# The last batch's output product by seven block products instead of eight, in an attention and gated projection kernel

## The chip, the cores and the metric

The kernel runs on one core of one Trainium2 chip. The metric is the time on the device in microseconds. The engines are PE (TensorE: matrix products), DVE (VectorE), ACT (ScalarE), POOL (GpSimd) and SP (SyncE, which issues most DMAs). "PEld" is PE's load of weights, which runs beside its products.

## The reference

```python
# q, k, v: (8 batches, 12 heads, 448 tokens, 64); x: (8, 448, 768)
scores = scale * q @ k.T - log(S)
attn = sigmoid(scores) @ v             # its heads side by side are x
gate = sigmoid(causal convolution of x over the tokens, 5 taps, each channel by itself)
val = x @ w_val                        # 768 x 768
out = (gate * val) @ w_out             # 768 x 768
```

All is float32.

## The kernel before

Everything is kept transposed: a row of 128 partitions holds 128 channels, and the columns are tokens. The 768 channels are six blocks, c for the summed side and m for the side that comes out. The tokens of batch 0 are spread over batches 1 to 7, so those have T = 448 + 64 = 512 columns each and batch 0 needs no products of its own.

The 48 pairs of heads are worked on in 24 steps j of two pairs each: scores on PE, a sigmoid on ACT (L552), scaling to float16 parts on ACT (`a`, L367) and DVE (L563), the product with v on PE (L602, L610). Three steps make a batch. The convolution (`tap`, `gate`) runs on ACT and DVE, with sums made by DMAs that POOL issues (L683).

A projection to near float32 accuracy is made of float16 numbers: each operand is a high part and a low part, and each 128 x 128 block takes three matmuls, hi by hi, hi by lo and lo by hi (L753). So a product for one m is 6 x 3 = 18 matmuls of 512 columns, summed in one of two PSUM banks (`ps_m`). For `val`, DVE multiplies the result with the gate (`y`, L777), a cast gives its high part and a difference its low part (`g`); for `out`, ACT or DVE scales the result (`y`) and two DMAs write it (L785 and L786). The last `out` product of the last batch is made in two halves of 256 columns (L759 to L769), so that the first half is written earlier. Weights come as 64-bit words, are made float32 in a buffer of the `words` ring (three buffers), get a power of two as scale from their largest value (`weight_sum`, a matmul with one column, L421; `exponent`), and are split (`weight_split`).

The order of the instructions isn't the order of the code. Each piece of work is an `op` with the engines that can do it, a cost on each, the buffers that it reads and writes, and a due time; the table AT holds the numbers that due times are made of. `Plan.issue` (L179) goes through a modelled time and gives each engine that comes free the ready op with the earliest due time. What comes out is one fixed list for each engine, and on the chip an engine executes its list in order. Buffers come from rings: an op that takes a buffer waits for the last reader of its former content.

After the last attention step PE has only products to do: `out` of batch 6, `val` of batch 7, `out` of batch 7, six column blocks each.

Of the kernel before, what the change touches and what calls it, by code (L numbers as in the profile page):

```python
# [58 lines left out]
VAL_SCALE = 2.0**-17  # L59
# [11 lines left out]
BY_GPSIMD = ()  # L71


# [5 lines left out]
    first=6.63, step=13.72, val=-77.5, val_step=60.94, out=57.5, out_step=597.15, w_max=-57.5,  # L79
    w_split=-155, load_qk_first=-152, load_qk=69.5, load_v=-40.5, split_hi=-2, split_lo=30,  # L80
    rest_first=95.5, rest=251, a_first=-174.5, a=-7, attend=-47.5, v_max=76.5, v_exp=14.5,
    v_split=-159.5, x=-174.5, x_max=-98, x_scale=-307, x_hi=52.5, x_lo=-185.5, x_step=2940.66, tap=51,
    scores=68.5, a_rest=85, a_rest_first=-72.5, tap_first=22, tap_pair=68.5, tap_step=56.18, gate=-110,
    product=63.5, y=-61.5, g_hi=186.5, g_lo=6, o=-97, share=0.3, w_load=-117,
# [172 lines left out]
def attention_then_gate(  # L257
# [101 lines left out]
    def copy(eng, to, x):  # L359
        if eng == "A":  # L360
            nc.scalar.copy(to, x)  # L361
        else:
            nc.vector.tensor_copy(to, x)
# [30 lines left out]
    def exponent(e, read, cols, prio, po=None):  # L394
# [24 lines left out]
    def weight_sum(n, m):  # L419
        b = w_max[n][m]  # L420
        return [b, ones], lambda to: mm(to[:, m : m + 1], ones(), b()[:, m : m + 1], start=True, stop=True)  # L421
# [313 lines left out]

    gv = {}

    def product(n, b, m):
        t = tau((b + 1) * NP) + AT["product"] + (m + NC * (n == "out")) * STEP / 2
# [19 lines left out]
        if (n, b, m) == ("out", B - 1, NC - 1):  # L759

            y = y_ring.new()
            for k, (low, cs) in enumerate(((y, slice(0, T // 2)), (y.part(), slice(T // 2, T)))):
# [4 lines left out]
                op({"S": 0.45}, t + k, lambda e, cs=cs: nc.sync.dma_start(out[b, m, :, cs], y()[:, cs]), [low], [], P * 1000)
            op({"S": 0.45}, t + 2, lambda e: nc.sync.dma_start(out[0, m, :, S - SL :], y()[:, S:]), [low], [], P * 1000)
# [70 lines left out]
    for j in range(TWOS):  # L839
        for i in (2 * j, 2 * j + 1):  # L840
            if i < len(columns):
                weight(*columns[i])
# [15 lines left out]
        if j + 1 < TWOS:  # L858
# [89 lines left out]
```

## Time and profile before

| | us |
|---|---|
| median of 3 runs | 579.45 |
| lowest and highest | 578.76, 580.03 |
| span of the profiled execution | 578.0 |
| PE busy | 571.4 |
| DVE busy | 428.4 |
| ACT busy | 435.4 |
| POOL busy | 138.2 |

The span is that of one profiled execution, from its first to its last instruction. A row of the timeline has start and duration in us, engine, line of the kernel, operation, output and inputs, shapes, and a count when neighbours are drawn together; in brackets stands the idle time before it and what ended that. In a group of instructions the first number behind the bar is their busy time in us, the second the mean of one in ns, the third the idle time before them. Matmuls are pipelined, so that their durations overlap: the pitch from start to start says what one costs.

### The profile page before, as it was taken

What the parts mean: (1) busy time and instruction counts of PE and PEld (TensorE: products, weight loads), DVE (VectorE), ACT (ScalarE), POOL (GpSimd) and SP (SyncE); (2) the same over time, 40 slices, a digit from 0 to 9 for tenths busy, and PEclk for the clock granted to TensorE, in tenths of its full rate; (3) what the DMA queues carried; (4) which work ended last, traced back from release to release, by engine and by line L of the source; (5) the groups of instructions that cost most, each with busy time, mean ns of one, the idle gap of its engine ahead of it and who ended that gap; (6) DMA issues with size and microseconds to landing.
All of it is one profiled execution on the core that took longest, in us unless ns stands there. A gap on an engine that the chain in (4) does not pass through costs nothing.

```text
span 578.0 us, 9459 instructions
## 1 busy us (share of the span) xinstructions
PE 571.4 (99%) x3592; PEld 280.2 (48%) x3592; DVE 428.4 (74%) x693; ACT 435.4 (75%) x579; POOL 138.2 (24%) x162
## 2 busy tenths in 40 slices
PE   9999999999999999999999999999999999999997
PEld 5343334455555555545555454554545555544444
DVE  1867999899977959888598886889777886760310
ACT  5677988879888869778697878788788897862112
POOL 0000203332424222243322333223322322110000
PEclk9999999999999999999999999999999999999999
DMA  8988677757484564825657364565635663355012
GB/s 327 355 279 267 174 210 188 203 120 184 124 215 83 146 157 141 207 58 155 136 158 176 102 169 96 166 156 155 169 74 168 155 133 74 72 128 129 2 37 74
DMA packets 39310, 88.44 MB, mean 153 GB/s; under 512 B 14944, under 2 KB 20448, under 8 KB 39264
## 3 DMA queue, kind: packets, MB, share of 16 engines
q0 software_dynamic: 8640, 31.46, 29.4%
q1 hardware_dynamic: 30624, 56.37, 28.9%
q8 instruction: 28, 0.46, 0.3%
q14 instruction: 18, 0.15, 0.1%
HBM read 43.96 MB, written 12.40 MB: 98 GB/s over the span
## 4 chain that ended last, share of the span: by engine, by line
PE 90%; DVE 5%; ACT 3%; DMA 1%; issue 1%; ACTq 0%; DVEq 0%
PE ps_m L753 54%; PE ps_a L516 15%; PE ps_a L610 14%; PE ps_a L539 3%; PE ps_a L602 2%; DMA gate<-tap 1%; ACT a_single L552 1%; DVE x_max L658 1%; DVE gate L679 1%; PE ps_m L800 1%; DVE a L563 1%; DVE w_words L389 1%; DVE out_max L415 0%; ACT tap L367 0%; ACT a L367 0%
## 5 line engine op out<-in xcount | busy, mean ns | idle before, releaser
L753 PE MATMUL ps_m<-g,w_out_hi 128*128 128x512 f16 (+1 forms) x516 | 150.5, 374 | 0.0
L753 PE MATMUL ps_m<-xs,w_val_hi 128*128 128x512 f16 x504 | 150.1, 379 | 0.0
L552 ACT ACTIVATE ps_a<-ps_a 128x896 f32<-128x896 f32 x112 | 99.3, 909 | 14.2 <-DVE v_exp L544 6.5
L563 DVE SCALAR_TENSOR_TENSOR a<-ps_a,a 128x896 f16<-128x896 f32 x96 | 100.8, 1082 | 7.0 <-ACT a L367 6.7
L372 POOL TENSOR_TENSOR qk_lo<-qk_src,qk_hi 128x448 fp32r<-128x448 f32 x66 | 75.2, 1151 | 119.8 <-ACT qk_hi L361 36.7
L753 PE MATMUL ps_m<-g,w_out_lo 128*128 128x512 f16 (+1 forms) x258 | 96.5, 374 | 0.0
L683 POOL DMA_DIRECT2D gate<-tap x60 | 53.5, 892 | 178.6 <-ACT tap L367 70.2
L753 PE MATMUL ps_m<-xs,w_val_lo 128*128 128x512 f16 x252 | 95.5, 379 | 0.0
L367 ACT ACTIVATE a<-ps_a 128x896 f16<-128x896 f32 x96 | 85.0, 927 | 0.2
L367 ACT ACTIVATE tap<-x,cw 128x512 f32<-128x512 f32 x120 | 82.2, 739 | 1.5 <-DMA gate<-tap 1.5
L753 PEld LDWEIGHTS <-w_out_hi 128*128 128x128 f16 x516 | 49.0, 98 | 59.6 <-issue 5.3
L753 PEld LDWEIGHTS <-w_val_hi 128*128 128x128 f16 x504 | 47.8, 98 | 61.1 <-issue 5.9
L777 DVE SCALAR_TENSOR_TENSOR y<-ps_m,y_scale,gate 128x512 f32<-128x512 f32 x42 | 29.9, 745 | 34.3 <-PE ps_m L753 34.3
L610 PE MATMUL ps_a<-a,v_hi 128*64 128x448 f16 x384 | 52.7, 354 | 0.0
L367 ACT ACTIVATE y<-ps_m,o_scale 128x512 f32<-128x512 f32 (+1 forms) x35 | 23.1, 678 | 38.0 <-PE ps_m L753 25.4
L552 ACT ACTIVATE a_single<-ps_a 128x896 f32<-128x896 f32 x56 | 48.0, 927 | 4.5 <-PE ps_a L516 4.1
L361 ACT CAST g<-y 128x512 f16<-128x512 f32 x28 | 17.2, 618 | 33.7 <-DVE y L777 32.9
L516 PE MATMUL ps_a<-qk_hi 64*128 64x448 f32 x198 | 39.8, 398 | 0.1
L753 PEld LDWEIGHTS <-w_out_lo 128*128 128x128 f16 x258 | 25.2, 98 | 29.2
L753 PEld LDWEIGHTS <-w_val_lo 128*128 128x128 f16 x252 | 24.7, 98 | 29.7
L516 PE MATMUL ps_a<-qk_single 64*128 64x448 f32 x180 | 39.0, 566 | 0.0
L610 PE MATMUL ps_a<-a_single,v_src 128*64 128x448 f32 x192 | 37.8, 543 | 0.0
(108 smaller groups left out, 752.9 us busy)
## 6 DMA issues: line engine op xcount, KB each, us to landing
gate<-tap POOLq DMA_DIRECT2D x60, 512.0 KB, 4.9
qk_src<-qk SPq DMA_DIRECT2D x33, 448.0 KB, 5.4
v_src<-vs SPq DMA_DIRECT2D x24, 448.0 KB, 4.3
out_t<-y SPq DMA_DIRECT2D x41, 224.0 KB, 3.1
qk_single<-qk SPq DMA_DIRECT2D x15, 448.0 KB, 5.9
w_words<-w_val SPq DMA_DIRECT2D x6, 768.0 KB, 8.1
w_words<-w_out SPq DMA_DIRECT2D x6, 768.0 KB, 5.4
x<-first_x SPq DMA_DIRECT2D x21, 68.0 KB, 4.2
```

The source lines that it names most:

```text
L361: nc.scalar.copy(to, x)
L367: nc.scalar.activation(to, x, AF.Copy, scale=by)
L372: engines[eng].tensor_tensor(to, x, y, op=ALU.subtract)
L516: mm(b()[:, h, :S], k()[rows, at : at + P], q()[rows, :S], start=(n == 0), stop=(n == len(terms(i)) - 1))
L539: mm(b()[to, h, :S], x[n]()[rows, CW:], x[n]()[rows, :S], start=True, stop=True)
L552: nc.scalar.activation(to, b()[:, :, :S], AF.Sigmoid, bias=-math.log(S), scale=1.0 / math.sqrt(D))
L563: op({"V": 1.0}, t + 0.5, lambda e: nc.vector.scalar_tensor_tensor(part(1), p(), A_SCALE, part(0), op0=ALU.mult, op1=ALU.subtract), [b], [ ...
L602: mm(px()[to, p, :S], v()[rows, h * D : (h + 1) * D], x(s["a"])[rows, h, at : at + S], start=(j > 0 and n == 0), stop=(j == 0 and n == len ...
L610: mm(px()[to, p, :S], v()[:, o : o + D], x(st[2 * j + p]["a", c])[:, h, at : at + S], start=(j == 0 and c == 0 and n == 0), stop=(j > 0 an ...
L683: op({"G": 1.1}, at + AT["tap_step"] * k, lambda e, tap=tap: nc.gpsimd.dma_start(g(), tap(), accum_op=ALU.add), [tap], [g], 4 * P * T * 4, "")
L753: mm(po()[:, cs], w()[:, c, :], x(k)[:, cs], start=(c == 0 and j == 0), stop=(c == NC - 1 and j == 2))
L777: op({"V": 0.66}, t + AT["y"], lambda e: nc.vector.scalar_tensor_tensor(y(), po(), y_scale()[:, m : m + 1], gate()[:, m % 2, :], op0=ALU.m ...
```

## The change

The tokens of the last batch are two halves of 256 columns, and the channels of the summed side (c even, c odd) and of the side that comes out (m even, m odd) are two blocks each. `out` of the last batch is then a 2 by 2 product of blocks, eight block products. The change makes it of seven (Strassen's algorithm):

- `mix(q)`, for each of the three pairs of column blocks of `w_out`: four sums and differences of blocks of weights, each 128 x 384, made from the high and low parts and split again. It takes a buffer of the `words` ring and two of the ring of `tap`. Its ops are due in mid-run (called at batch 4), on DVE, POOL and ACT. For this the two blocks of a pair share one scale (`weight_sum`: four matmuls of one column for a pair, instead of two).
- The last batch's `val` result is multiplied with the gate in place (L912). `form(b, q)` splits three blocks, adds blocks in place (four adds of 128x256, L813), and splits the four blocks that come out.
- `product_mixed(b)`: seven steps of three q of three c of three matmuls of 256 columns (L852), into both halves of a bank of `ps_a`, with an evacuation of 256 columns after each step of each q that scales and adds or subtracts (L871, L369), and DMAs to the output.
- Two `out` products of batch 6 (HELD_BACK = 2, m = 4 and 5) are due after `val` of batch 7.
- The table of due times is new throughout, due times are rounded to five digits, BY_GPSIMD (empty) is gone.

The core of the diff:

```diff
-VAL_SCALE = 2.0**-17
+VAL_SCALE = 2.0**-19
+OUT_TOP = 13
+HELD_BACK = 2
 AT = dict(
-    first=6.63, step=13.72, val=-77.5, val_step=60.94, out=57.5, out_step=597.15, w_max=-57.5,
+    first=-11.29, step=17.95, val=156.55, val_step=-46.86, out=18.08, out_step=-29.96, w_max=90.21,
...
+    w_load=192.46, mix=196.26, mix_step=-137.47, form=63.29, mixed=64.39, held=-170.35,
 )
...
     def weight_sum(n, m):
-        b = w_max[n][m]
-        return [b, ones], lambda to: mm(to[:, m : m + 1], ones(), b()[:, m : m + 1], start=True, stop=True)
+        b = w_max[n][m : m + (1 if n == "val" else 2)]
+
+        def emit(to):
+            for at in range(m, m + len(b)):
+                for k, x in enumerate(b):
+                    mm(to[:, at : at + 1], ones(), x()[:, m + k : m + k + 1], start=(k == 0), stop=(k == len(b) - 1))
...
+    def mix(q):
+        prio = AT["mix"] + AT["mix_step"] * q
+        f = mixed[q] = words.new(lambda: sb.tile([P, 8, NQ * P], F16, name="mixed", tag="w_words", bufs=WORDS))
+        t, u = tap_ring.new(), tap_ring.new()
...
+        def two_sub(to, k, a, b, at):
+            op({"G": 1.05, "V": 0.45}, prio + at, lambda e: sub(e, slot(to, k), block(0, *a), block(0, *b)), reads, [to])
+            op({"G": 1.05, "V": 0.45}, prio + at, lambda e: sub(e, slot(u, 1), block(1, *a), block(1, *b)), reads, [u])
+            op({"G": 1.05, "V": 0.45}, prio + at, lambda e: engines[e].tensor_tensor(
+                flat(to, k), flat(to, k), flat(u, 1), op=ALU.add), [u], [to])
...
+        def split(n, src, k, sign, at):
+            op({"A": 0.5, "V": 0.32}, prio + at, lambda e: scaled(e, hi(), flat(src, k), sign), [src], [part[n]])
...
+    def form(b, q):
+        g, t = st[b * NP + 2 * q]["g"], tau((b + 1) * NP) + AT["form"] + 2 * q
...
+            op({"A": 0.2 + 0.21 * n, "V": 0.1 + 0.16 * n}, t, lambda e, at=at, n=n, to=to: copy(
+                e, h()[:, to : to + n, :], blocks()[:, at:, :]), [g], [hb])
+            op({"V": 0.1 + 0.3 * n, "G": 0.2 + 0.62 * n}, t + 0.1, lambda e, at=at, n=n, to=to: sub(
+                e, l()[:, to : to + n, :], blocks()[:, at:, :], h()[:, to : to + n, :]), [g, hb], [lb])
+            if at:
+                def add(e):
+                    x = blocks()
+                    for a, by in ((2, 0), (0, 1), (1, 2), (3, 1)):
+                        engines[e].tensor_tensor(x[:, a, :], x[:, a, :], x[:, by, :], op=ALU.add)
+                op({"V": 1.5}, t + 0.2, add, [], [g])
...
+    def product_mixed(b):
+        steps = (
+            (0, 0, "B11", True), (1, 5, 0, True), (0, 4, 1, False), (1, 6, "B22", False), (0, 3, 2, False),
+            (1, 2, "B21", True), (0, 1, 3, False),
+        )
...
+                        for j, (a, src) in enumerate(((0, h), (0, l), (1, h))):
+                            mm(acc[q][0]()[:, bank, :HT], stat[a](), src()[:, f, :], start=(first and c == 0 and j == 0),
+                               stop=(c == NQ - 1 and j == 2), skip_group_check=True)
+                    op({"P": 0.327}, at + c * 0.01, emit, [*src, *reads], [x])
...
-        if (n, b, m) == ("out", B - 1, NC - 1):
-            y = y_ring.new()
-            for k, (low, cs) in enumerate(((y, slice(0, T // 2)), (y.part(), slice(T // 2, T)))):
-                po = columns(cs, t + k * STEP / 4)
...
+        if n == "val" and b == B - 1:
+            g = st[b * NP + m]["g"]
+            op({"V": 0.66}, t + AT["y"], lambda e: nc.vector.scalar_tensor_tensor(
+                g()[:, m % 2, :], po(), y_scale()[:, m : m + 1], g()[:, m % 2, :], op0=ALU.mult, op1=ALU.mult), [po, y_scale], [g], port="")
+            if m % 2:
+                form(b, m // 2)
+            return
...
-            for m in range(NC):
+            for m in range(NC - (HELD_BACK if b == B - 1 else 0)):
                 product("out", b - 1, m)
         for m in range(NC):
             product("val", b, m)
-    for m in range(NC):
-        product("out", B - 1, m)
+        if b == 4:
+            for q in range(NQ):
+                mix(q)
+    for m in range(NC - HELD_BACK, NC):
+        product("out", B - 2, m, AT["held"])
+    product_mixed(B - 1)
```

What the order makes of it is shown at two places. The first is PE at the end of `val` of batch 7. Before, the last matmuls of the sixth block (`w_val_hi_78`, `w_val_lo_90`) stand between matmuls of `out` of the same batch (`w_out_hi_79`, its first block):

```order
L753 LDWEIGHTS w_val_hi_78
L753 MATMUL ps_m<-xs,w_val_hi_78 128x512
L753 LDWEIGHTS w_val_lo_90
L753 MATMUL ps_m<-xs,w_val_lo_90 128x512
L753 LDWEIGHTS w_out_hi_79
L753 MATMUL ps_m<-g_5713,w_out_hi_79 128x512
```

After, the same two are followed by a piece of the mixed product (L852, `form_hi` and `form_lo` being the split blocks of the gated value) and then by the first of the two held products of batch 6 (`w_out_hi_83`, its fifth block):

```order
L902 LDWEIGHTS w_val_hi_78
L902 MATMUL ps_m<-xs,w_val_hi_78 128x512
L902 LDWEIGHTS w_val_lo_90
L902 MATMUL ps_m<-xs,w_val_lo_90 128x512
L852 LDWEIGHTS w_out_hi_81
L852 MATMUL ps_a<-form_hi,w_out_hi_81 128x256
L852 MATMUL ps_a<-form_lo,w_out_hi_81 128x256
L852 LDWEIGHTS w_out_lo_93
L852 MATMUL ps_a<-form_hi,w_out_lo_93 128x256
L902 LDWEIGHTS w_out_hi_83
L902 MATMUL ps_m<-g,w_out_hi_83 128x512
```

So 36 matmuls of batch 6, and pieces of the mixed product that need only the first two pairs of blocks, now stand between the last `val` product and the first matmul that reads the last blocks' sums.

The second place is DVE in mid-run, in a step of attention, from the gating of two `val` products to the step's `x_max`. Before:

```order
L777 SCALAR_TENSOR_TENSOR y<-ps_m,y_scale,gate 128x512 x2
L372 TENSOR_TENSOR g<-y,g 128x512
L544 TENSOR_SCALAR v_exp<-ps_a 128x1
L573 TENSOR_SCALAR v_exp<-v_exp 128x1
L575 TENSOR_SCALAR v_exp<-v_exp 128x1
L577 TENSOR_SCALAR v_exp<-v_exp 128x1
L563 SCALAR_TENSOR_TENSOR a_rest<-ps_a,a_rest 128x2x448
L369 TENSOR_SCALAR v_hi<-v_src,v_exp 128x896
L583 SCALAR_TENSOR_TENSOR v_lo<-v_src,v_exp,v_hi 128x896
L658 TENSOR_REDUCE x_max<-x 128x2
```

After, in a step where sums of weights are made (`tap` and `mixed` are here the buffers that mix takes):

```order
L922 SCALAR_TENSOR_TENSOR y<-ps_m,y_scale,gate 128x512 x2
L374 TENSOR_TENSOR g<-y,g 128x512
L552 TENSOR_SCALAR v_exp<-ps_a 128x1
L581 TENSOR_SCALAR v_exp<-v_exp 128x1
L374 TENSOR_TENSOR tap<-w_out_hi_81,w_out_hi_82 128x384
L374 TENSOR_TENSOR tap<-w_out_lo_93,w_out_lo_94 128x384
L583 TENSOR_SCALAR v_exp<-v_exp 128x1
L571 SCALAR_TENSOR_TENSOR a_rest<-ps_a,a_rest 128x2x448
L371 TENSOR_SCALAR mixed<-tap 128x384
L371 TENSOR_SCALAR v_hi<-v_src,v_exp 128x896
L374 TENSOR_TENSOR mixed<-tap,mixed 128x384
L666 TENSOR_REDUCE x_max<-x 128x2
```

Four instructions of mix stand here on DVE, two of them ahead of `a_rest`, and `v_lo` has moved behind this stretch; in the three steps together there are 31 of them on DVE.

More of the change, by code (lines that the diff above doesn't have):

```diff
@@ L57 @@
 WN = NC * P
-VAL_SCALE = 2.0**-17
+VAL_SCALE = 2.0**-19
+OUT_TOP = 13
+HT = T // 2
+NQ = NC // 2
+HELD_BACK = 2
 WORDS = 3
@@ L68 @@
 LATER = 6
-BY_GPSIMD = ()
 ADDED_FIRST = 2
@@ L78 @@
 AT = dict(
-    first=6.63, step=13.72, val=-77.5, val_step=60.94, out=57.5, out_step=597.15, w_max=-57.5,
[L80 to L84, printed above, removed]
+    first=-11.29, step=17.95, val=156.55, val_step=-46.86, out=18.08, out_step=-29.96, w_max=90.21,
+    w_split=-122.85, load_qk_first=-99.99, load_qk=-179.16, load_v=-105.08, split_hi=-3.23, split_lo=335.04,
+    rest_first=239.77, rest=218.39, a_first=-163.54, a=-78.86, attend=-109.14, v_max=28.54, v_exp=-192.36,
+    v_split=-38.2, x=-182.91, x_max=-214.54, x_scale=-616.43, x_hi=-131.74, x_lo=111.42, x_step=95.05,
+    tap=-37.37, scores=116.22, a_rest=31.92, a_rest_first=-22.47, tap_first=159.05, tap_pair=335.08,
+    tap_step=35.74, gate=16.21, product=-134.09, y=-167.06, g_hi=72.06, g_lo=294.15, o=59.1, share=0.13,
+    w_load=192.46, mix=196.26, mix_step=-137.47, form=63.29, mixed=64.39, held=-170.35,
 )
@@ L392, in convert, with exponent @@
             e, high().bitcast(F32), high().bitcast(F32), REBIAS), [], [t])
-    def exponent(e, read, cols, prio, po=None):
+    def exponent(e, read, cols, prio, po=None, top=V_TOP):
         op({"V": 0.08}, prio, lambda _: nc.vector.tensor_scalar(
@@ new lines, in parts_of @@
+    def parts_of(b):
+        return [b, *b.parts]
+    forms = {}
+    def form(b, q):
+        g, t = st[b * NP + 2 * q]["g"], tau((b + 1) * NP) + AT["form"] + 2 * q
+        h = a_ring.new(lambda: sb.tile([P, 7, HT], F16, name="form_hi", tag="a", bufs=a_ring.n))
+        l = a_ring.new(lambda: sb.tile([P, 7, HT], F16, name="form_lo", tag="a", bufs=a_ring.n))
+        h2, l2 = h.part(), l.part()
+        forms[q] = ((h, l), (h2, l2))
+        blocks = lambda: g().rearrange("p c (t n) -> p (c t) n", t=2)
+        for (hb, lb), at, n, to in (((h, l), 1, 3, 0), ((h2, l2), 0, 4, 3)):
+            op({"A": 0.2 + 0.21 * n, "V": 0.1 + 0.16 * n}, t, lambda e, at=at, n=n, to=to: copy(
[8 more added lines that the diff above has]
+                op({"V": 1.5}, t + 0.2, add, [], [g])
@@ L736, in attention_then_gate, with product @@
     gv = {}
-    def product(n, b, m):
-        t = tau((b + 1) * NP) + AT["product"] + (m + NC * (n == "out")) * STEP / 2
+    def product(n, b, m, late=0.0):
+        t = tau((b + 1) * NP) + AT["product"] + (m + NC * (n == "out")) * STEP / 2 + late
         h, l = w_hi[n, m], w_lo[n, m]
@@ L842, in attention_then_gate @@
                 weight(*columns[i])
-                if i < NC + EARLY:
+                if i < NC:
                     weight_split(*columns[i])
+                elif i == NC + 1:
+                    weight_split("out", 0)
         if j == 0:
@@ L865, in attention_then_gate @@
                 then.append(lambda b, n=j // 3: x_scale(n, b))
-            for m in range(EARLY, NC):
+            for m in range(EARLY, NC, 2):
                 if j == LATER + (m - EARLY) // 2:
@@ L893, in attention_then_gate @@
             product("val", b, m)
-    for m in range(NC):
-        product("out", B - 1, m)
+        if b == 4:
+            for q in range(NQ):
+                mix(q)
+    for m in range(NC - HELD_BACK, NC):
+        product("out", B - 2, m, AT["held"])
+    product_mixed(B - 1)
     plan.close(rings)
```

110 lines of the change are left out of this document (92 added, 18 removed).

## The prediction

> **What bounds the kernel now.** I read the waits of PE first, then windows of the span, then the chain of waits from 520 us. The waits of PE, whole span (sum in us, how often, the longest):
>
> ```profile
> PE ps_m L800 <- DVE ones L793: 1.1, 1, 1.1
> PE ps_a L702 <- ACT diagonal L367: 0.9, 1, 0.9
> PE ps_a L539 <- ACT a_single L552: 0.7, 2, 0.4
> ```
>
> The windows (length, then busy us and instructions of PE, PEld, DVE, ACT, POOL, the granted clock, DMA):
>
> ```profile
> 0.00:50.00 50.00, 48.60 (x291) 20.84 (x293) 29.50 (x59) 34.27 (x41) 1.81 (x14) 1.00 0.89 314
> 50.00:92.00 42.00, 40.65 (x226) 14.91 (x223) 39.02 (x71) 36.60 (x50) 7.63 (x10) 1.00 0.74 211
> 92.00:574.20 482.20, 482.09 (x3079) 244.47 (x3077) 359.91 (x565) 364.06 (x489) 128.75 (x139) 1.00 0.54 132
> 117.00:142.30 25.30, 25.19 (x169) 12.94 (x168) 24.31 (x44) 21.96 (x29) 7.92 (x8) 1.00 0.64 144
> 340.00:389.60 49.60, 49.60 (x334) 25.51 (x334) 41.00 (x64) 41.32 (x56) 14.42 (x17) 1.00 0.56 135
> ```
>
> The chain at the end (start, us, what):
>
> ```profile
> 520.00 54.24 PE ps_m L753 x269
> 574.23 0.02 issue
> 574.26 0.47 ACT y L367
> ```
>
> The kernel is a stream of matmuls. PE idles 2.75 us before 92 us (1.40 and 1.35 in the first two windows), 0.11 us from there to 574.20, and the clock is full throughout. So a matmul that disappears shortens the run by its pitch, if its successors have their operands in time. The other engines matter only where they hold PE up.
>
> **The pitch.** The timeline at the end, where `out` of the last batch runs in 512 and in 256 columns (start, duration):
>
> ```profile
> 557.17 0.59 PE L753 MATMUL ps_m<-g,w_out_hi 128*128 128x512 f16 x2
> ...
> 567.53 0.59 PE L753 MATMUL ps_m<-g,w_out_hi 128*128 128x512 f16 x2
> ...
> 571.43 0.38 PE L753 MATMUL ps_m<-g,w_out_hi 128*128 128x256 f16 x2
> 571.54 0.10 PEld L753 LDWEIGHTS <-w_out_lo 128*128 128x128 f16 x1
> ...
> 573.73 0.38 PE L753 MATMUL ps_m<-g,w_out_hi 128*128 128x256 f16 x2
> ```
>
> Durations overlap, so I go by starts. From 557.17 to 567.53 lie 16 groups of three matmuls of 512 columns: 10.36 / 48 = 0.2158 us each. From 571.43 to 573.73 lie 7 groups of three of 256: 2.30 / 21 = 0.1095 us each. The weight load takes 0.10 us and is hidden under the 0.11 us of a 256-column matmul, though barely. The Trainium skill, "TensorE: Matmul & The Clock Gate", The mechanism, has a load overlap a running matmul only if the two differ in row group; these all use 128 rows, so it speaks against narrow matmuls. The trace disagrees: load and matmul would follow each other at 0.10 + 0.11 = 0.21 us, and start 0.1095 us apart.
>
> **Part 1, the product by seven (L852).** Removed: five column blocks of 18 matmuls of 512 columns and one of 36 of 256: 90 x 0.2158 + 36 x 0.1095 = 19.42 + 3.94 = 23.36 us. Added: 7 x 3 x 3 x 3 = 189 matmuls of 256 columns: 189 x 0.1095 = 20.70 us. All lie on the path, which here is PE alone. **-2.66 us.** The rest of PE's matmuls is the same in number, but for six one-column sums of weight maxima (18 for 12). Their row:
>
> ```profile
> L421 PE MATMUL ps_a<-out_max,ones 128*128 128x1 bf16 x4 | 0.4, 165 | 0.0
> ```
>
> Six of them cost between 0 and 6 x 0.165 = 1.0 us; the 0.165 is a latency that the pipeline mostly covers, as in the 0.59 for two matmuls above, so I take **+0.2 us**.
>
> **Part 2, the seam.** Sums of blocks of the gated value (form) are made after each pair of the last `val` products, and the mixed product needs them. The last `val` product ends, then its gating, hi, lo, four adds, hi and lo follow in a chain. The rows nearest to these, and the load of DVE at this place today:
>
> ```profile
> L777 DVE SCALAR_TENSOR_TENSOR y<-ps_m,y_scale,gate 128x512 f32<-128x512 f32 x42 | 29.9, 745 | 34.3 <-PE ps_m L753 34.3
> L372 DVE TENSOR_TENSOR g<-y,g 128x512 f16<-128x512 f32 x36 | 24.6, 687 | 3.8 <-ACT g L361 3.4
> L361 ACT CAST g<-y 128x512 f16<-128x512 f32 x28 | 17.2, 618 | 33.7 <-DVE y L777 32.9
> ```
> ```profile
> 520.00:540.00 20.00, 20.00 (x94) 9.11 (x93) 3.31 (x5) 4.86 (x7) 0.91 (x2) 1.00 0.41 97
> 540.00:560.00 20.00, 20.00 (x95) 9.01 (x94) 5.77 (x8) 3.79 (x6) 0.00 (x0) 1.00 0.04 13
> ```
>
> Scaled by elements: 0.75 + 0.93 + 1.03 (768 wide) + 4 x 0.40 (256 wide, between 0.34 and 0.69) + 1.24 + 1.37 (1024 wide) = 6.9 us. PE's cover after that `val` product is the order's: two held products, 36 x 0.2158 = 7.8 us, and eight pieces of the first two steps at 0.33 us, 2.6 us, before the first matmul that reads the last sums: 10.4 us, so 3.5 to spare. Without the held products the stall would be 6.9 - 2.6 = 4.3 us. DVE is idle for over 70% of these windows. The last gate (L693 on ACT) is the other input; its cover is about 1 us, since the bank that the first held product takes is released by that gating. I take 0 for the seam, and up to 1.5 us for a late gate.
>
> **Part 3, the tail.** Today an evacuation of 256 columns, a DMA of 96 KB and one of 32 KB behind it; then the evacuation and one DMA of 128 KB.
>
> ```profile
> 574.76 0.33 SPq L767 DMA_DIRECT2D out_t<-y  x1
> 575.14 0.42 SPq L768 DMA_DIRECT2D out_t<-y  x1
> ```
> ```profile
> out_t<-y SPq DMA_DIRECT2D x4, 32.0 KB, 1.8
> out_t<-y SPq DMA_DIRECT2D x1, 128.0 KB, 1.9
> ```
>
> 575.14 + 1.8 = 576.94 against 574.76 + 1.9 = 576.66: between -0.3 and +0.3, I take 0.
>
> **Part 4, the sums of weights in mid-run (mix).** No PE work, so nothing if it fits into idle time. The place is three steps of 24.8 us, from about 315 to 390 us. A step's x_max on DVE:
>
> ```profile
> 340.50 1.21 DVE L658 TENSOR_REDUCE x_max<-x 128x2 f32<-128x1024 f32 x1
> 365.32 1.21 DVE L658 TENSOR_REDUCE x_max<-x 128x2 f32<-128x1024 f32 x1
> ```
>
> There DVE idles (49.60 - 41.00) / 2 = 4.3 us per step, 12.9 in three. In the order, the same stretch loses on DVE two g casts, two qk_hi casts, one xs and two g differences, and gains a gate and a y; by these rows
>
> ```profile
> L363 DVE CAST g<-y 128x512 f16<-128x512 f32 x14 | 7.7, 571 | 0.1
> L363 DVE CAST qk_hi<-qk_src 128x384 fp32r<-128x384 f32 x24 | 15.6, 650 | 0.0
> L369 DVE TENSOR_SCALAR xs<-x,x_exp 128x1024 f16<-128x1024 f32 x12 | 9.5, 822 | 0.2
> L369 DVE TENSOR_SCALAR gate<-x,cw 128x512 f32<-128x512 f32 x22 | 10.1, 478 | 0.0
> L369 DVE TENSOR_SCALAR y<-ps_m,o_scale 128x512 f32<-128x512 f32 x8 | 6.0, 746 | 2.2 <-PE ps_m L753 2.2
> ```
>
> it loses 1.14 + 1.30 + 0.82 + 1.37 - 0.48 - 0.75 = 3.4 us. Room: 16.3 us. Added are 31 mix instructions of 128x384. Lower price 0.687 x 384 / 512 = 0.515, upper 0.687 (the whole 512-wide g difference); neighbours overlap by some 0.06 us, as below: 31 x (0.455 to 0.627) = 14.1 to 19.4 us. At 0.55 it is 15.2: DVE about 98% busy. The nearest stretch is 117 to 142.3: DVE 24.31 of 25.30 (96%), PE lost 0.11. So I take 0.2 us per step, **+0.6 us**, bounds 0 and 5.0 (below). Mix instructions also wait on each other across DVE, ACT and POOL, and behind one that waits on ACT stands the sigmoid that PE's next scores need.
>
> What makes the upper end possible is POOL:
>
> ```profile
> 342.02 0.35 DVE L363 CAST qk_hi<-qk_src 128x384 fp32r<-128x384 f32 x1
> ...
> 349.51 0.69 DVE L372 TENSOR_TENSOR g<-y,g 128x512 f16<-128x512 f32 x1
> 351.11 0.68 DVE L372 TENSOR_TENSOR g<-y,g 128x512 f16<-128x512 f32 x1
> 351.29 1.50 POOL L372 TENSOR_TENSOR qk_lo<-qk_src,qk_hi 128x448 fp32r<-128x448 f32 x1 [1.98 <-DVE qk_hi L363]
> 351.71 1.29 DVE L363 CAST qk_hi<-qk_src 128x384 fp32r<-128x384 f32 x1
> 353.08 1.00 POOL L372 TENSOR_TENSOR qk_lo<-qk_src,qk_hi 128x384 fp32r<-128x384 f32 x1 [0.29 <-DVE qk_hi L363]
> ```
>
> The same cast takes 0.35 us alone and 1.29 beside a POOL instruction; the two-input difference takes 0.69 alone and 0.68 beside it. The Trainium skill, "GPSIMD Engine Reference", Specifications, has the two engines share their SBUF interfaces, with contention for VectorE instructions in a two-port mode or with two SBUF inputs. The cast agrees, the difference doesn't.
>
> **The sum** against the profiled run: -2.66 + 0.2 + 0.6 = -1.86 us, span 578.0 to 576.1. The median lies 1.45 us over the span (launch and end, untouched): 579.45 - 1.86 = **577.6 us**.
>
> **Rivals.** Less than 0.2% (1.16 us: 578.29 to 580.61) can't be told from no change.
>
> 1. As forecast, with stalls of 0 to 1.2 us and sums of 0 to 0.5: 576.8 to 578.3. Chance 0.54.
> 2. The new due times also cure the head. Of PE's 2.75 us there, 1.6 stand at L702 and L539. PE's order in the head is nearly unchanged, which speaks against. Half of it: 577.6 - 0.8 = 576.8, all of it 576.0. Chance 0.09.
> 3. The saving is half eaten: steps with mix cost PE 0.6 to 1 us each, or the last gate comes 1.5 us late. Total stalls 1.3 to 3.6; at 2.4 us: 579.45 - 2.66 + 0.2 + 2.4 = 579.4. For it: DVE at 98% in an order without slack. Chance 0.20.
> 4. Slower: DVE becomes the bound of the three mix steps. At the upper price it needs 19.4 of 16.3, 3.1 us over; and POOL gets 14 mix instructions of about 1.03 us, 14.4 of 74.4 us, so of some ten casts and scalings on DVE two more meet POOL, at 1.29 - 0.35 = 0.94: 1.9. Together 5.0 us: 579.45 - 2.46 + 5.0 = 582.0. It decides from 3.6 us of stalls (2.46 + 1.16), or 1.2 us per step. Against: between 117 and 142 us PE hardly suffered. Chance 0.13.
> 5. Two-input instructions on DVE wait for POOL after all. POOL would be busy with 14 mixes and some 12 differences, 27 of 74.4 us or 36%; 28 of DVE's 31 have two inputs: 28 x 0.36 x 0.94 = 9.5 us over 1.1 of spare: 579.45 - 2.46 + 8.4 = 585.4. This is the second half of the Trainium skill's rule above; the 0.68 speaks against it. Chance 0.02.
> 6. The change doesn't do what it says: 189 matmuls bound by their loads at 0.21 us take 39.7 us, 19 more than forecast, 596.6. The 7 groups above speak against it. Chance 0.02.
>
> Faster is 1 and 2: 0.63. Same is 3: 0.20. Slower is 4 to 6: 0.17. The forecast is the likeliest case's. The range takes in cases 1 to 3 with their bounds, 575.8 to 580.6; the likeliest case alone has 576.8 to 578.3.
>
> **What would show it.** Right: L852 x189 at 0.1095 us from start to start, about 20.7 us in sum; no PE wait over 0.3 us for form_hi, form_lo or gate after 507 us; DVE about 97% busy between 315 and 390 us, PE there idle for less than 1 us; the head as before. Wrong: PE waits of a microsecond for a, a_rest or qk in the mix steps (cases 3, 4); DVE's tap and mixed instructions well over 0.55 us (4, 5); PE waiting for the last gate (3); a pitch over 0.12 us at L852 (6).

## The result

The changed kernel takes 589.03 us (median of 5 runs, 587.09 to 589.78) against 579.37 (578.76 to 580.03) of the kernel before on the same chip: ratio 1.0165 [1.015, 1.018]. The forecast was 577.6, with a range of 575.8 to 580.6. It was wrong by 11.4 us and in its sign. The profiled execution is the shortest of the five, with a span of 585.3 us; the other four have 587.0 to 587.9, so some 2 us of the median's loss stand in no trace.

The page of the changed kernel, its busy times and its chain:

```profile
PE 569.7 (97%) x3661; PEld 285.9 (49%) x3661; DVE 465.0 (79%) x741; ACT 432.9 (74%) x579; POOL 164.1 (28%) x183
PE 57%; DVE 33%; ACT 6%; issue 3%; POOL 0%; DVEq 0%; ACTq 0%; POOLq 0%
```

PE's busy time fell by 1.7 us (571.4 before), and yet the span grew by 7.3. In the chain of the kernel before PE had this share:

```profile
PE 90%; DVE 5%; ACT 3%; DMA 1%; issue 1%; ACTq 0%; DVEq 0%
```

So DVE went from 5% of the chain to 33%. What PE waits for, now (sum in us, times, longest):

```profile
PE ps_a L524 <- DVE a_rest L571: 2.9, 4, 1.5
PE ps_a L710 <- ACT diagonal L369: 1.7, 1, 1.7
PE ps_m L902 <- DVE xs L740: 1.6, 1, 1.6
...
PE ps_a L524 <- ACT x L369: 1.1, 1, 1.1
```

POOL is named nowhere, and its share of the chain is 0%. Windows of a hundred us, first of the kernel before, then of the changed one (length, then busy us and count of PE, PEld, DVE, ACT, POOL, the granted clock, DMA):

```profile
0.00:100.00 100.00, 97.25 (x560) 40.10 (x562) 76.52 (x141) 76.63 (x99) 12.19 (x27) 1.00 0.81 258
100.00:200.00 100.00, 99.89 (x642) 49.92 (x640) 88.15 (x148) 86.22 (x116) 32.46 (x34) 1.00 0.63 154
200.00:300.00 100.00, 100.00 (x674) 51.86 (x672) 79.05 (x123) 82.02 (x110) 30.60 (x33) 1.00 0.58 142
```

```profile
0.00:100.00 100.00, 94.91 (x563) 39.87 (x564) 79.08 (x144) 73.91 (x93) 12.45 (x23) 1.00 0.73 245
100.00:200.00 100.00, 97.89 (x634) 49.07 (x633) 89.30 (x138) 83.58 (x112) 32.93 (x38) 1.00 0.65 156
200.00:300.00 100.00, 98.85 (x660) 50.63 (x659) 82.11 (x128) 83.81 (x114) 33.71 (x37) 1.00 0.65 154
300.00:400.00 100.00, 97.93 (x649) 49.66 (x649) 96.27 (x149) 74.70 (x104) 45.20 (x44) 1.00 0.44 116
400.00:500.00 100.00, 99.39 (x663) 50.79 (x662) 78.83 (x122) 82.47 (x111) 32.97 (x36) 1.00 0.61 139
500.00:570.00 70.00, 69.99 (x407) 36.53 (x404) 35.10 (x55) 33.06 (x47) 6.88 (x8) 1.00 0.39 83
```

From 300 us on PE idled nowhere before (the prediction's window from 92 us). By rows, PE's new idle time is 2.34 + 2.00 + 1.15 + 2.07 + 0.61 + 0.01 = 8.2 us. Only the fourth row holds weight sums; 5.5 us of the loss lie before 300 us, where the change, but for six short sums of weight maxima, only moves work.

One of these stalls in full. The chain through 225 to 240 us (start, us, what):

```profile
229.68 2.77 DVE xs L740
...
232.78 0.07 DVE v_exp L552
...
232.88 0.91 ACT ps_a L560
...
233.81 0.92 ACT a_rest L369
...
236.92 0.90 ACT x L369
...
237.86 0.87 PE ps_a L524 x6
```

And the timeline there:

```profile
227.41 1.27 DVE L740 SCALAR_TENSOR_TENSOR xs<-x,x_exp,xs 128x1024 f16<-128x1024 f32 x1
...
229.45 0.87 POOL L691 DMA_DIRECT2D gate<-tap  x1 [0.61 <-ACT tap L369]
...
229.61 2.85 DVE L740 SCALAR_TENSOR_TENSOR xs<-x,x_exp,xs 128x1024 f16<-128x1024 f32 x1
230.06 1.30 POOL L374 TENSOR_TENSOR qk_lo<-qk_src,qk_hi 128x384 fp32r<-128x384 f32 x1
...
232.88 0.90 ACT L560 ACTIVATE ps_a<-ps_a 128x896 f32<-128x896 f32 x1 [2.12 <-DVE v_exp L552]
...
237.86 0.47 PE L524 MATMUL ps_a<-qk_hi 64*128 64x448 f32 x2 [1.08 <-ACT x L369]
```

The same kind of DVE instruction, `xs` of one shape, takes 1.27 us at 227.41 and 2.85 at 229.61; its end, 232.46, is 1.10 us behind the end of POOL's difference, 231.36. Behind it in DVE's list stands `v_exp`, for which the sigmoid on ACT waits 2.12 us, and at the end of that row PE waits 1.08. None of these instructions is new. Only their place is. By its rows this case isn't quite clean: `xs` began 0.45 us ahead of POOL's difference, but 0.16 us behind a DMA issue of POOL (L691). In e5 below POOL's DMA issues stay, its differences read nothing, and no such instruction is held; which of the two held `xs` first the rows don't tell.

The other stalls look alike. PE has five gaps of over 1 us in the changed kernel: 1.69 us from 76.1, 1.58 from 97.3, 1.17 from 127.9, 1.08 from 236.8 and 1.50 from 362.0. Up to 8 us ahead of each, on the chain that ended last, stand DVE instructions that ran beside a difference of POOL and took longer than the shortest of their form: by 1.8, 1.8, 2.0, 1.6 and 1.5 us in sum.

The instruction on which the prediction's argument stood shows the same. The `g` difference, unhindered and held:

```profile
197.60 0.69 DVE L374 TENSOR_TENSOR g<-y,g 128x512 f16<-128x512 f32 x1
...
198.68 1.17 POOL L374 TENSOR_TENSOR qk_lo<-qk_src,qk_hi 128x448 fp32r<-128x448 f32 x1 [5.80 <-DVE qk_hi L365]
198.78 1.62 DVE L374 TENSOR_TENSOR g<-y,g 128x512 f16<-128x512 f32 x1
```

At 198.78 POOL had begun 0.10 us earlier: DVE's difference ends at 200.40, that is 0.55 us behind POOL's end at 199.85. In the row of the prediction, DVE's difference began at 351.11 and POOL's at 351.29, so DVE was first. Over all of DVE's rows, 21 instructions of the kernel before are more than 0.15 us longer than others of their form, by 14.9 us in sum; in the changed kernel 34, by 27.0 us.

### The profile page after: what moved, and what is told of

Same layout as the page of the kernel before. It is cut to its first block, busy times and chain, and to the rows that moved or that the text cites. A ratio compares the mean times of both kernels' runs of the same rounds, so it can differ in the third digit from the quotient of the medians.

```text
span 585.3 us, 9634 instructions
## 1 busy us (share of the span) xinstructions
PE 569.7 (97%) x3661; PEld 285.9 (49%) x3661; DVE 465.0 (79%) x741; ACT 432.9 (74%) x579; POOL 164.1 (28%) x183
## 4 chain that ended last, share of the span: by engine, by line
PE 57%; DVE 33%; ACT 6%; issue 3%; POOL 0%; DVEq 0%; ACTq 0%; POOLq 0%
PE ps_m L902 32%; PE ps_a L524 9%; PE ps_a L618 8%; DVE a L571 6%; PE ps_a L852 4%; DVE gate L687 3%; DVE xs L740 3%; PE ps_a L547 2%; ACT ps_a L560 2%; DVE x_max L666 2%; DVE y L922 1%; PE ps_a L610 1%; DVE gate L371 1%; DVE qk_hi L365 1%; DVE w_words L391 1%
## 5 line engine op out<-in xcount | busy, mean ns | idle before, releaser
L902 PE MATMUL ps_m<-g,w_out_hi 128*128 128x512 f16 x432 | 128.7, 379 | 0.0
L374 POOL TENSOR_TENSOR qk_lo<-qk_src,qk_hi 128x448 fp32r<-128x448 f32 x66 | 80.5, 1228 | 124.9 <-DVE qk_hi L365 89.4
L691 POOL DMA_DIRECT2D gate<-tap x60 | 52.5, 875 | 139.7 <-ACT tap L369 69.9
L369 ACT ACTIVATE tap<-x,cw 128x512 f32<-128x512 f32 x120 | 85.4, 733 | 6.7 <-DMA gate<-tap 6.7
L369 ACT ACTIVATE a<-ps_a 128x896 f16<-128x896 f32 x96 | 85.2, 921 | 0.0
L902 PE MATMUL ps_m<-g,w_out_lo 128*128 128x512 f16 x216 | 81.9, 379 | 0.0
L902 PEld LDWEIGHTS <-w_out_hi 128*128 128x128 f16 x432 | 40.9, 98 | 51.4 <-issue 5.2
L524 PE MATMUL ps_a<-qk_hi 64*128 64x448 f32 x198 | 40.8, 408 | 4.2 <-DVE a_rest L571 2.9
L363 ACT CAST g<-y 128x512 f16<-128x512 f32 x31 | 19.0, 617 | 28.7 <-DVE y L922 28.4
L687 DVE SCALAR_TENSOR_TENSOR gate<-x,cw,gate 128x512 f32<-128x512 f32 x48 | 38.7, 816 | 0.0
L524 PE MATMUL ps_a<-qk_single 64*128 64x448 f32 x180 | 37.1, 550 | 0.0
L524 PE MATMUL ps_a<-qk_lo,qk_hi 64*128 64x448 f32 x198 | 36.3, 362 | 0.0
L524 PE MATMUL ps_a<-qk_hi,qk_lo 64*128 64x448 f32 x198 | 36.2, 362 | 0.0
```

The source lines that it names most:

```text
L369: nc.scalar.activation(to, x, AF.Copy, scale=by)
L374: engines[eng].tensor_tensor(to, x, y, op=ALU.subtract)
L524: mm(b()[:, h, :S], k()[rows, at : at + P], q()[rows, :S], start=(n == 0), stop=(n == len(terms(i)) - 1))
L687: op({"V": 0.67}, at + AT["tap_step"] * k + AT["tap_pair"] * p, lambda e, p=p, part=part, k=k: nc.vector.scalar_tensor_tensor(part(), x()[ ...
L691: op({"G": 1.1}, at + AT["tap_step"] * k, lambda e, tap=tap: nc.gpsimd.dma_start(g(), tap(), accum_op=ALU.add), [tap], [g], 4 * P * T * 4, "")
L902: mm(po()[:, cs], w()[:, c, :], x(k)[:, cs], start=(c == 0 and j == 0), stop=(c == NC - 1 and j == 2))
```

## The experiments

Three theories were weighed. **Due times**: the new table puts old work into worse places, whatever DVE and POOL do to each other. **Load**: the sums of weights fill DVE. **Meeting**: DVE instructions with two inputs in SBUF wait while POOL reads SBUF, and in the new order that falls ahead of what PE needs.

**e1_old_due and e8_old_due_scaled: the changed kernel with the old table.** The entries that both tables have are the old ones; in e8 the new entries are fitted to it as well.

```diff
-    first=-11.29, step=17.95, val=156.55, val_step=-46.86, out=18.08, out_step=-29.96, w_max=90.21,
+    first=6.63, step=13.72, val=-77.5, val_step=60.94, out=57.5, out_step=597.15, w_max=-57.5, w_split=-155,
...
+    share=0.3, w_load=-117, mix=196.26, mix_step=-137.47, form=63.29, mixed=64.39, held=-170.35,
```

> The changed kernel with the old table of due times for all entries that the old table has (mix, mix_step, form, mixed and held keep the new values). The changed kernel's trace has PE waits of about 9 us that the old one hasn't: 1.75 at 96.9 us, 1.33, 0.70 and 0.63 between 127 and 136, 1.34 at 236, 1.75 at 362, 0.68 at 388, 0.86 at 464. Theory 1 (the new due times are to blame: they let DVE and POOL meet, or put work late): all but those of the mix steps go, 579.4 - 2.5 + 0 to 2.5 = 577 to 579.5 us. Theory 2 (the mix work overfills DVE, whatever the due times): most of the loss stays, 585 us or more.

> As the run with the old table of due times (603.5 us), but with the new entries moved to the same place in the run: there mix = 196 was ten steps of pairs too early on the old table's scale (step 13.72 for 17.95), so that the mix ops went ahead of everything once their buffers were free. Here mix is 333, mix_step -105, form 48.4, mixed 49.2, held -130. If that was why the old table was slow, the waits of 2.9, 2.9, 3.8 and 2.4 us between 405 and 460 go: 580 to 590 us. If the old table does not fit the new ops in itself: 598 us or more.

Measured: e1 603.45 us, ratio 1.0425 [1.0372, 1.0477]; e8 597.94, ratio 1.0308 [1.0276, 1.034]. What due times expected of e1 is missed by far, and e8 lies just under the 598 us expected if the old table doesn't fit. The waits of PE in e1:

```profile
PE ps_a L543 <- DVE a L570: 8.4, 3, 3.4
PE ps_m L901 <- DVE y L921: 5.3, 4, 2.1
```

The added work does not fit into the old order: DVE is late for `a` and `y`, in gaps of up to 3.4 us. So these two say that the change needed another table, and not what the new one costs.

**e2_before_new_due: the kernel before with the new table**, without its new entries.

> The old kernel with the new table of due times and nothing else of the change; no product by seven, no mix. Theory 1 (due times): the waits outside the mix steps appear here too, 6 to 7 us: 585 to 587 us. Theory 2 (mix): 579 to 580 us, as before.

Measured: 583.51 us, ratio 1.0076 [1.0058, 1.0094]. That lies between the two expectations, 585 to 587 and 579 to 580. The table alone costs 4.4 us, on a kernel in which nothing else changed. Its PE was busy 96.58, 99.38 and 68.36 us in the windows 0 to 100, 100 to 200 and 500 to 570, and throughout in the others: PE's new idle time is 0.7 + 0.5 + 1.6 = 2.8 us. So the table costs something on old work alone, but less than half of what is to be explained; and its order of the old work isn't quite that of the changed kernel, whose list of work is another.

**e4_mix_out: the sums of weights are not issued**, and the product reads fills, or a copy of a block, in their place.

```diff
-            op({"G": 1.05, "V": 0.45}, prio + at, lambda e: sub(e, slot(to, k), block(0, *a), block(0, *b)), reads, [to])
+            op({"G": 1.05, "V": 0.45}, prio + at, lambda e: None, reads, [to])
```

> The changed kernel with its order, but the 30 sums and differences of weights aren't issued, and the parts of the sums are filled with zeros or with a copy of a block; the weights' sums are left out. Theory 1 (due times): only the waits in the mix steps go, 2.4 us of the 9: 589.0 to 586.5. Theory 2 (mix overfills DVE and the delay is passed on): 5 us or more go, 584 or less.

Measured: 584.97 us, ratio 1.01 [1.0083, 1.0117]. That lies between the two expectations again. The sums of weights cost 4.1 us by the medians, and 1.9 between the two profiled executions (585.3 and 583.4 us). The stretch that held them:

```profile
300.00:400.00 100.00, 100.00 (x665) 51.07 (x664) 83.57 (x134) 77.05 (x107) 31.87 (x34) 1.00 0.46 122
```

PE is whole there again, while ahead of 300 us it idles as much as in the changed kernel. Load, by itself, explains at most these 4.1 us.

**e3_pool_short: POOL's differences become fills.** The order is that of the changed kernel, instruction by instruction; POOL's 84 differences (`qk_lo`, `g`, parts of the weight sums) write zeros and read nothing. Those low parts are left out.

```diff
     def sub(eng, to, x, y):
+        if eng == "G":
+            return nc.gpsimd.memset(to.bitcast(F32) if to.dtype == F32R else to, 0.0)
         engines[eng].tensor_tensor(to, x, y, op=ALU.subtract)
```

> The changed kernel with the same order on every engine, but each of POOL's 84 subtractions and sums that go through the common subtraction helper writes zeros instead (a fill), so POOL is busy for a shorter time and reads nothing; the low parts that POOL makes are left out. Theory 1a (meeting: a DVE instruction with two inputs in SBUF, or a cast, that starts while POOL runs waits for POOL's end; 27.0 us of such excess in the changed kernel, 14.9 in the old): the excess falls below 8 us and with it PE's waits at 236, 362 and 464; 589 to about 583 or less. Theory 1b (the new order is late by itself): at most 1 us less, 588.

Measured: 577.28 us, ratio 0.9964 [0.9951, 0.9977]. That is 11.8 us below the changed kernel and faster than the kernel before.

**e5_pool_two_fills: two fills in place of each difference**, so that POOL is busy nearly as long. The same low parts are left out.

```diff
+        if eng == "G":
+            to = to.bitcast(F32) if to.dtype == F32R else to
+            nc.gpsimd.memset(to, 0.0)
+            return nc.gpsimd.memset(to, 0.0)
```

> The run with POOL's subtractions as fills (577.3 us) took 11.8 us off the changed kernel. Two readings: POOL's reading of SBUF no longer holds DVE up (meeting), or POOL is simply done earlier (580 ns a fill for 1.15 to 1.3 us) and whoever waits for it starts earlier (latency). Here each is two fills in a row, so that POOL is busy as long as with the subtraction but reads nothing; the low parts that POOL makes are left out as there. Meeting: 576.5 to 579 us, DVE's two-input instructions at their undisturbed 0.69, 0.74 and 1.27 us beside a fill. Latency: back to 585 us or more.

Measured: 576.73 us, ratio 0.9952 [0.9934, 0.997]. Two of its windows, to be held against those of the changed kernel above:

```profile
100.00:200.00 100.00, 100.00 (x642) 50.50 (x642) 85.99 (x139) 84.23 (x115) 34.22 (x62) 1.00 0.66 157
...
300.00:400.00 100.00, 100.00 (x680) 51.33 (x670) 92.05 (x151) 77.65 (x107) 39.98 (x71) 1.00 0.45 122
```

POOL is busy 34.22 us between 100 and 200, more than the 32.93 of the changed kernel, and PE idles nowhere. So it isn't that POOL is busy; it is what POOL reads, or what it waits for. For a fill needs no input: in the changed kernel POOL's `qk_lo` waits 89.4 us in sum for DVE's `qk_hi`, in e5 not at all, so that its results also come earlier. That late results of POOL stall PE has no sign in the changed kernel, where no wait of PE names POOL and POOL's share of the chain is 0%, but e5 by itself doesn't exclude it. No DVE instruction with two tensors in SBUF as inputs is held by over 0.15 us here; casts and scalings beside fills still are (a `qk_hi` cast takes 0.65 to 0.70 us in place of 0.35), and PE loses nothing by that. And between 300 and 400 us DVE holds old work and weight sums in 92.05 us without a stall: the load alone would have fitted.

**e6_before_pool_short: the same edit as in e3 on the kernel before**, as a control, with its `qk_lo` and `g` low parts left out.

> The old kernel with the same edit (POOL's 72 subtractions are fills; those low parts are left out). Its trace has 14.9 us of excess on DVE by POOL, but PE hardly waits after 92 us. If meetings cost only where DVE has no slack: 578 to 579 us, at most 1 us less than the old kernel, and the changed kernel with fills is 1.5 to 2.5 us faster than this. If the fills help every kernel by the same: 567 to 570 us.

Measured: 578.89 us, ratio 0.9994 [0.9985, 1.0004]: nothing. In the old order the meetings, 14.9 us on DVE, lay where there was slack.

**e10_qk_fill and e11_rest_fill: the fills for one group each.** In e10 only `qk_lo` (66 instructions) is a fill, in e11 only the others (`g` and weight sums); that low part is left out each time.

```diff
+        if eng == "G" and to.dtype == F32R:
+            return nc.gpsimd.memset(to.bitcast(F32), 0.0)
```

> The changed kernel with fills only for POOL's 66 differences for the scores (qk_lo, which the old kernel has as well; that low part is left out); POOL's g and mix work stays. Of the 27.0 us of excess on DVE, some 21 lie beside qk_lo. If the old work in a new place is what hurts: 577 to 580 us. If the added work on POOL (13 g for 6, 14 mix) hurts: 585 us or more.

> The counterpart: fills only for the differences of g and of mix that POOL makes (their low parts left out), qk_lo as it is. Old work in a new place: 585 to 588 us, at most 4 us less than the changed kernel. Added work: 580 us or less.

Measured: e10 577.99 us, ratio 0.9974 [0.9964, 0.9984]; e11 586.21, ratio 1.0123 [1.0104, 1.0143]. Old work does it: the differences of `qk_lo`, which the change doesn't touch, are worth 589.03 - 577.99 = 11.0 us; POOL's share of the weight sums and of `g` is worth 2.8. They don't add up to e3's 11.8 (perhaps some stalls have a partner of each kind; that wasn't looked into).

**e7_pool_qk_only: POOL keeps `qk_lo` alone**, its other work goes to DVE, and the order is made anew.

```diff
-            op({"G": 1.17, "V": 0.6}, t + AT["g_lo"], lambda e: sub(e, g()[:, 1, :], y(), g()[:, 0, :]), [y], [g])
+            op({"V": 0.6}, t + AT["g_lo"], lambda e: sub(e, g()[:, 1, :], y(), g()[:, 0, :]), [y], [g])
```

> The changed kernel with POOL as an engine taken away from the sums of weights and from the low part of g: POOL keeps only the 66 subtractions for the scores, DVE gets the other 26 (13 x 0.69 + 14 x 0.55 = 16.7 us more in the whole run), and the order is planned anew by the same table. Meeting: fewer two-input instructions of DVE meet POOL, excess from 27 to 20 us or less, 583 to 587 us. Load: in the mix steps DVE is at 96 to 98% already and gets 7.7 us more, so 591 us or more.

Measured: 599.13 us, ratio 1.0337 [1.0312, 1.0363]. A miss: what meeting expected is not what came. The stretch with the sums of weights:

```profile
300.00:400.00 100.00, 92.45 (x623) 46.79 (x623) 98.20 (x168) 74.70 (x103) 27.68 (x25) 1.00 0.41 109
```

DVE is full there and PE loses 7.55 us. So load is real as a limit (the prediction's rival 4), though the changed kernel stays short of it: sparing meetings by giving DVE more work costs more than it brings.

**e9_micro: the meeting by itself.** The kernel before, with rounds of four equal DVE instructions added behind 553 us: first with POOL idle, then beside 14 differences of POOL in a row. They are added work, so only the rows count:

```profile
555.67 2.54 DVE L908 TENSOR_TENSOR u<-u,u 128x448 f32<-128x448 f32 x4
558.12 1.67 DVE L910 CAST uh<-u 128x448 f16<-128x448 f32 x4
559.71 1.26 DVE L912 SCALAR_TENSOR_TENSOR u<-ps_a,u 128x128 f32<-128x128 f32 x4
560.88 2.58 DVE L916 TENSOR_REDUCE uh<-u 128x1 f16<-128x448 f32 x4
...
563.80 4.44 DVE L908 TENSOR_TENSOR u<-u,u 128x448 f32<-128x448 f32 x4
563.85 15.40 POOL L921 TENSOR_TENSOR u<-u 128x448 f32<-128x448 f32 x14 [39.25 <-DVE u L919]
568.16 4.24 DVE L910 CAST uh<-u 128x448 f16<-128x448 f32 x4
572.32 1.25 DVE L912 SCALAR_TENSOR_TENSOR u<-ps_a,u 128x128 f32<-128x128 f32 x4
573.49 2.58 DVE L916 TENSOR_REDUCE uh<-u 128x1 f16<-128x448 f32 x4
```

> The old kernel with added work on idle engines behind the last attention step, on buffers of its own: on DVE four instructions each of a difference with two SBUF inputs (128x448 float32), a cast (128x448 to float16), one that reads PSUM and SBUF (128x128), and a maximum with one SBUF input; then the same sixteen again while POOL makes 14 differences of 128x448 in a row. Meeting: first round about 0.6, 0.35, 0.3 and 0.6 us each; second round the differences and the casts wait for POOL's instruction in progress, 1.2 us or more each, the other two kinds as in the first. If what held DVE up in the traces was something else than POOL's reading: second round like the first.

Four differences with two inputs in SBUF go from 2.54 to 4.44 us. The first of them began at 563.80, ahead of POOL, so three are held, by (4.44 - 2.54) / 3 = 0.63 us each: the length of one of them, as if the two engines took turns. Four casts go from 1.67 to 4.24, or 1.06 each, a little under the 1.2 us expected. An instruction that reads PSUM and SBUF stays at 1.25, a maximum over one input at 2.58.

**e12_turns_kept: the changed kernel with a third table**, all arithmetic kept. The table is chosen so that DVE's instructions with two inputs, where PE's next operands stand behind them, and POOL's differences fall apart in time.

```diff
-    first=-11.29, step=17.95, val=156.55, val_step=-46.86, out=18.08, out_step=-29.96, w_max=90.21,
+    first=-16.26, step=24.56, val=-58.83, val_step=-591.73, out=-185.97, out_step=36.32, w_max=127.04,
...
+    w_load=141.79, mix=224.43, mix_step=-141.24, form=31.87, mixed=493.39, held=694.22,
```

> The changed kernel with nothing but another table of due times, all arithmetic kept. The table was chosen so that, with the durations of these traces and with DVE and POOL taking turns wherever a DVE instruction is of the kinds that waited in the small measurement, no turn is waited for just ahead of something that PE needs. Meeting as the cause: about the time of the changed kernel with fills (576.7 to 577.3 us), 576 to 579, below the old kernel's 579.4. If something else in the product by seven cost the time (its mix work, its seam), no table helps: 585 us or more.

Measured: 579.69 us, ratio 1.0006 [0.9996, 1.0016]: 9.3 us below the changed kernel, level with the kernel before, and 0.7 us over the range that was expected (576 to 579). Its windows:

```profile
0.00:100.00 100.00, 95.01 (x556) 39.55 (x556) 75.82 (x134) 71.94 (x92) 9.30 (x22) 1.00 0.73 240
100.00:200.00 100.00, 99.67 (x647) 50.27 (x644) 89.48 (x143) 87.77 (x118) 41.36 (x41) 1.00 0.66 161
200.00:300.00 100.00, 100.00 (x668) 51.42 (x667) 79.66 (x126) 87.56 (x120) 32.33 (x37) 1.00 0.66 157
300.00:400.00 100.00, 100.00 (x667) 51.39 (x665) 90.62 (x147) 80.48 (x112) 43.42 (x43) 1.00 0.45 118
```

With POOL's reading in place and the product by seven in place, PE idles 0.33 us from 100 to 400 (and not at all from there to 570). On DVE 22 instructions are still held, by 15.9 us in sum, as in the kernel before: not the number of meetings counts, but, as it seems, their place. As the whole table is another, e12 shows that an order without the loss in mid-run exists, and can't by itself tell meetings from all else that an order sets. What keeps it from the forecast is the head: 97.25 - 95.01 = 2.2 us more idle time there than before, about what the product saves. Its PE waits there for `diagonal` (1.8 us, L710) and for `x` (0.9, L524). Whether an order can have both, a head as before and this mid-run, wasn't tried; in e10, in the changed kernel's order with `qk_lo` as fills, PE is busy for 97.70 us of the head.

## Why the prediction was wrong, by its own steps

- **What bounds the kernel**: right as a statement with a condition ("if its successors have their operands in time"). The condition failed, and no part of the sum priced it outside the three steps with weight sums.
- **Part 1, the product**: right. In the changed kernel the matmul of L852 that starts at 575.02 and the one at 577.31 are 21 starts apart: 2.29 / 21 = 0.109 us. With POOL's reading out, e10, e3 and e5 give 577.99, 577.28 and 576.73 around the 577.6 of the sum; e5 lies 2.57 us below the kernel before beside it (579.30), where -2.66 + 0.2 were forecast. That the totals come so close is in part luck: in these three runs the head is 0.4 us better than before, and the tail (below) 0.5 to 1.4 us longer.
- **Part 2, the seam**: right. PE is busy for 69.99 of the 70 us from 500 to 570; no wait for `form` or the last gate shows.
- **Part 3, the tail**: a term mis-sized, taken as 0, at most 0.3. From PE's last start to the end of the span there were 578.0 - 573.95 = 4.05 us and are 585.3 - 580.48 = 4.82, so +0.77. The last rows of SP and ACT:

```profile
579.89 1.22 SPq L882 DMA_DIRECT2D out_t<-y_mixed  x1
```

```profile
L882 SPq DMA_DIRECT2D out_t<-y_mixed x6: 332/338/1222, 573.8 to 582.0; - x6
```

```profile
580.79 0.47 ACT L369 ACTIVATE y_mixed<-ps_a,o_minus 128x256 f32<-128x256 f32 x1 [0.18 <-PE ps_a L852]
```

  The last piece is ready at 581.26; its DMA is issued at 582.0, because the first of the last three issues took 1.22 us in place of 0.34 and the others queue behind it. Six issues (L876 and L878) stand ahead of it within 3 us, which the prediction didn't count. And this run got off lightly: in five other runs that end with the mixed product, one of the tail's issues takes 1.57 to 2.32 us, and the stretch from PE's last start is 4.56 us (e3), 5.11 (e5), 5.46 (e10), 5.79 (e4) and 5.93 (e11). The term is 0.5 to 1.9 us, not 0.
- **Part 4, the weight sums**: a size. +0.6 was taken, within bounds of 0 and 5.0; e4 shows 4.1 (1.9 between profiled executions). DVE was read rightly as nearly full: it was busy for 73.93 of the 75 us from 315 to 390, where 98% was forecast. PE idled 2.0 us there, where less than 1 was, but it isn't DVE's full load that stalls it: e5 has the same work and no stall.
- **The step that failed** stands at the end of part 4: "the two-input difference takes 0.69 alone and 0.68 beside it", and with it rival 5, "the 0.68 speaks against it. Chance 0.02". The row was misread. DVE's difference at 351.11 was under way when POOL's began at 351.29; the row says what happens when DVE comes first. The row that decides is one in which POOL's start is ahead of DVE's, and the trace of the kernel before has it, outside the rows that the prediction shows:

  ```profile
  395.36 1.00 POOL L372 TENSOR_TENSOR qk_lo<-qk_src,qk_hi 128x384 fp32r<-128x384 f32 x1
  395.92 0.98 DVE L679 SCALAR_TENSOR_TENSOR gate<-x,cw,gate 128x512 f32<-128x512 f32 x1
  ...
  396.83 0.74 DVE L679 SCALAR_TENSOR_TENSOR gate<-x,cw,gate 128x512 f32<-128x512 f32 x1
  ```

  `gate` has two inputs in SBUF. Begun 0.56 us behind POOL's difference it took 0.98 us and ended 0.54 us behind POOL's end; the next of its form took 0.74. The same stands at 246.88, 321.40 and 470.44. So the evidence for rival 5 lay in the trace, and it deserved a large chance. The Trainium skill, "GPSIMD Engine Reference", Specifications, had the rule right, both halves: e9 shows casts and two-input instructions held alike (1.67 to 4.24 and 2.54 to 4.44 us).
- **Rival 5's size**: it gave 585.4, 3.6 short of 589.03, because it counted new instructions only, in three steps. e10 and e11 show that the larger part is old work, `qk_lo` on POOL against `xs`, `g` and `gate` on DVE, in the whole run. "The head as before" failed for the same reason: a new table moves all work, also where nothing is added. e2 prices this for the old work at 4.4 us.
- **Rival 1's bounds**: with its own 0.5 and 1.2 us it ends at 578.5, not at 578.3; nothing hangs on it.
- **Rivals 2, 3 and 6**: the head got worse, by 2.34 us of PE; in e10 that loss is gone, so it too goes with POOL's `qk_lo`. There was no late gate. Loads did not bound the product.

So the causal account is: product, seam and pitch as forecast (-2.5 us); meetings of DVE with POOL's reads, placed ahead of PE's operands by the new order, +11.0 to +12.3 us (the size from e3, e5 and e10, with e6 as control, the mechanism from e9 and the rows ahead of PE's gaps, and e12 for the placement; open is what share of it the fills gain by not waiting for inputs); of this, up to 4.1 need the weight sums (e4); and +0.8 in the tail, whose cause, the long issue, was read from the traces alone. With e3's 11.8 the sum is 579.37 - 2.5 + 11.8 + 0.8 = 589.5, against 589.03.

## What to carry to other kernels

A row that shows two engines side by side decides about contention only if the one in question started second: look at the start times before reading a duration as "unhindered". When an order is made anew, price the old work too: list which instructions of DVE stand ahead of PE's next operand, and which of POOL's reads can fall on them. An engine can hold another up without appearing in any list of waits: it shows as one instruction with two durations.

## What the runs showed of the hardware that was not expected

- DVE and POOL take turns, and the one that is under way finishes. Held instructions ended 0.55 us (of 0.69) and 0.54 us (of 0.74) behind POOL's end, at 198.78 and in the kernel before at 395.92. Eight `g` differences of the kernel before began 0.18 to 0.23 us ahead of POOL's, and all took 0.68 or 0.69 us. POOL pays too: in e9 its differences take 1.36 and 1.19 us beside DVE's, and 0.93 at the least. The Trainium skill, "VectorE: DVE Perf Modes", in its section on two Vector instructions with no wait between them, says what goes through the read interface that GpSimd shares: the second of two SBUF inputs, or the input in a two-port mode. By that rule the instruction with PSUM and SBUF and the maximum over one input should be free, and in e9 they are (1.26 and 1.25, 2.58 and 2.58).
- The clock of PE fell after one gap of 2.4 us. Windows of e1, a us each:

```profile
77.00:78.00 1.00, 0.00 (x0) 0.00 (x0) 1.00 (x2) 0.29 (x1) 0.88 (x1) 1.00 1.20 344
78.00:79.00 1.00, 0.00 (x0) 0.00 (x0) 1.00 (x5) 0.40 (x2) 0.00 (x0) 1.00 0.76 301
...
80.00:81.00 1.00, 1.00 (x4) 0.50 (x4) 0.80 (x3) 1.00 (x2) 0.00 (x0) 0.50 0.96 217
...
82.00:83.00 1.00, 1.00 (x5) 0.14 (x2) 1.00 (x3) 0.95 (x2) 0.00 (x0) 0.50 0.91 257
```

  Three us at a granted clock of 0.50 (80 to 83) cost another 1.5 us of matmuls, by estimate. The Trainium skill, "TensorE: Matmul & The Clock Gate", Part 1, has the half clock after an idle window of about 3.4 us; here PE was idle for 0.31 + 1 + 1 + 0.06 = 2.4 us (0.69 busy from 76 to 77, 0.94 from 79 to 80). The length of a gap alone doesn't decide it here: in the same run two gaps of 2.5 us (from 405.7 and from 426.3) left the clock at 1.00, and in e7 it fell to 0.50 at 467 us, behind a gap of 1.4 us (from 464.3). The changed kernel's gaps, up to 1.7 us, left it at 1.00 in all windows above.
- A DMA issue of SP took 1.22 us where its like took 0.34, behind six others in 3 us; in e3, e4, e5, e10 and e11 one of the last issues took 1.57 to 2.32. What sets this off was not tried.
